# A recurrent attention with two expert layers: scans two chunks ahead, the last gate as three and one, and weight splits placed elsewhere

## Chip, core and metric

The kernel runs on one core of a Trainium2 chip, in one launch. The metric is the time of one execution on the device in microseconds, lower is better; the time given is the median of the runs, with the lowest and the highest beside it.

## The reference

Three layers follow each other. First a recurrence over 768 tokens for each of 4 batches and 8 heads of 48 channels:

```python
for t in range(S):
    cur = einsum('bhd,bhe->bhde', u * k[t], v[t])
    y[t] = einsum('bhd,bhde->bhe', r[t], state + cur)
    state = w[t] * state + einsum('bhd,bhe->bhde', k[t], v[t])
```

Its output is taken as 3072 tokens of 384 values. Each token whose skip score is positive goes through one of 8 experts, the one with the largest logit, and the result is scaled by the softmax weight and added:

```python
h = maximum(x[mask] @ w1[e], 0)          # 384 -> 1024
out[mask] = x[mask] + gate_w * (h @ w2[e])
```

A dense layer follows: `h = x @ w_in` (384 to 2048), `g = h * clip(h + 3, 0, 6) / 6`, `out = g @ w_out`.

## The kernel before

The order of each engine's instructions is written out by hand: what stands in the source is what the engine gets, in that order, and each engine works its own list from front to back, waiting where an input isn't ready or a buffer isn't free. There are three stages.

**The recurrence** works on 24 chunks (`NST`): 6 blocks of 128 tokens, 4 batches in each; chunk i is block i // 4 of batch i % 4. A loop over i holds in one step the work of several chunks:

- DVE: `state(i - 1)` updates the batch's state (lines 569 and 573, from the fifth step on), with the forward scan of a later chunk between its two lines (`scan`, line 431); then `scan_end`, `scan_inv` and four backward scans (`scan_back`, line 446); `masked(i + 1, 0)` and `(i + 1, 1)`, which mask the two groups of scores (line 494); the output add of chunk i in `x_out` (line 546, tile xt).
- POOL: `scale(i + 2)` multiplies r and k by the scanned weights (line 456, tile rkt); line 470 in `scale_rest`; the scatters of tokens to the experts' lists (line 663), of chunk i - 7.
- PE: `scores(i + 1)` (line 490, out of rkt), `apply(i)` in two halves (lines 524 to 534), with the transposes of chunk i - 1 between them (`xpose`), `k_xpose(i + 1)`, `state_mm(i)`, and the logits of chunk i - 1.
- ACT: copies, and `diag_v(i)`.

The state update reads the PSUM bank that the logits are written to as well, so it waits for the logits of the step before. Scores go to two banks, one for each group, and a group's next scores wait until the mask has read the last. Each block has a gate, in four functions: `gate_a` (six small instructions on DVE) and `gate_rank` (PE) in one step, `gate_o` and `gate_b` (DVE) in the next. The last block's gate runs as two halves of two chunks.

The experts' weights are split into a high part, which ACT rounds (`w_hi`, line 270), and a low part, which is the difference (`w_lo`, line 276). Twelve pieces of 128x768, the first expert's eight and four of the second's, are split within the recurrence: one in each of the steps 9 to 20, the low part on POOL. Raw pieces come in by DMA two steps ahead (`w_raw`).

**The experts**: for each of 8, eight pairs of `ffn1` and `ffn2`. A table of positions (`side_at`) places the splits of the coming expert between them, and work on the dense layer's weights: `d_words`, `d_bits`, `d_value`, `d_hi` and `d_lo` (line 327, on DVE). At the end of an expert, DVE adds its outputs to the tokens (line 855) and POOL scatters them back.

**The dense block**: 6 blocks of 512 tokens, PE without a gap.

Warm-up matmuls (`warm1`, line 394) fill PE at the start; their results are not used.

## Time and profile before

| what | before |
|---|---|
| median of 3 runs | 760.0 us (758.72 to 761.14) |
| the profiled execution | 762.69 us, span 761.0 us |
| mean granted clock of TensorE | 0.988 |
| PE busy | 734.3 us, 96% |
| DVE busy | 497.3 us, 65% |
| ACT busy | 346.9 us, 46% |
| POOL busy | 219.0 us, 29% |
| chain that ended last | PE 69%, DVE 21%, DMA 3% |

The share of busy time is a mean over three stages with different limits, and a busy PE is not one that PE's peak bounds, since the ends of matmuls are modelled. The chain of waits goes back from the last instruction, at each step to what released it; stretches of the timeline show who waited for whom in one place.

### The profile page before, as it was taken

The numbers are of one execution on the slowest core, as the hardware profiler recorded it, in microseconds if no ns is written. First come the engines' busy times: TensorE is split into PE (matmuls) and PEld (weight loads), VectorE is DVE, ScalarE is ACT, GpSimd is POOL, SyncE is SP. The second block draws the span as 40 slices with busy tenths as digits, with TensorE's granted clock in tenths as the row PEclk, the third lists the DMA queues.
The fourth block names the chain that finished last, engine by engine and source line by source line (L and its number), as shares of the span: only waits on it lengthen the run. The fifth ranks groups of instructions, "written<-read, shape, count | busy, mean of one in ns | idle before, by whom it ended". The sixth has DMA issues, their size and how long they took to land.

```text
span 761.0 us, 14589 instructions
## 1 busy us (share of the span) xinstructions
PE 734.3 (96%) x5653; PEld 604.8 (79%) x5653; DVE 497.3 (65%) x974; ACT 346.9 (46%) x796; POOL 219.0 (29%) x192
## 2 busy tenths in 40 slices
PE   7999999989999997989999999999999999999995
PEld 3788888859999997957777888888888888788884
DVE  8989999837999999927885454455445434333331
ACT  2666777626566666326554333333233333333331
POOL 3758999942344444303441000000000000000000
PEclk9999999999999999989999999999999999999998
DMA  8699888328787873042230220221022010001001
GB/s 233 206 300 264 246 243 251 112 86 287 249 276 238 288 250 143 13 159 62 85 103 13 77 68 13 79 66 37 2 90 67 25 54 1 1 0 43 0 1 46
DMA packets 40590, 90.84 MB, mean 119 GB/s; under 512 B 5442, under 2 KB 19552, under 8 KB 40512
## 3 DMA queue, kind: packets, MB, share of 16 engines
q1 hardware_dynamic: 37952, 85.14, 36.6%
q0 software_dynamic: 2560, 4.69, 1.7%
q8 instruction: 46, 0.75, 0.4%
q14 instruction: 32, 0.26, 0.1%
HBM read 72.51 MB, written 20.53 MB: 122 GB/s over the span
## 4 chain that ended last, share of the span: by engine, by line
PE 69%; DVE 21%; DMA 3%; ACT 2%; issue 2%; SPq 1%; POOL 0%; DVEq 0%; ACTq 0%
PE f L787 8%; PE f L788 8%; PE f L790 8%; PE acc L950 8%; PE acc L952 8%; PE acc L949 8%; DVE wlo L276 5%; PE sc L490 4%; PE x L534 3%; PE x L529 3%; PE x L524 2%; DVE wlo L327 2%; DVE hl L828 2%; DVE a L304 2%; DVE a L307 2%
## 5 line engine op out<-in xcount | busy, mean ns | idle before, releaser
L935 DVE SCALAR_TENSOR_TENSOR f<-t,f 128x512 f32<-128x512 f32 x96 | 66.6, 694 | 130.5 <-ACT t L934 130.5
L934 ACT ACTIVATE t<-f,three 128x512 f32<-128x512 f32 x96 | 66.0, 688 | 160.1 <-PE f L790 160.1
L950 PE MATMUL acc<-gh,wlo 128*128 128x512 f32 x288 | 115.0, 399 | 2.0 <-DVE wlo L327 1.8
L787 PE MATMUL f<-bh,whi 128*128 128x512 f32 x288 | 115.6, 401 | 0.6 <-ACT bh L922 0.6
L949 PE MATMUL acc<-gh,whi 128*128 128x512 f32 x288 | 115.7, 402 | 0.0
L788 PE MATMUL f<-bh,wlo 128*128 128x512 f32 x288 | 115.1, 400 | 0.0
L937 DVE TENSOR_TENSOR gl<-f,gh 128x512 fp32r<-128x512 f32 x96 | 66.4, 691 | 63.8 <-ACT gh L936 63.8
L936 ACT ACTIVATE gh<-f 128x512 fp32r<-128x512 f32 x96 | 57.4, 598 | 100.3 <-DVE f L935 100.3
L952 PE MATMUL acc<-gl,whi 128*128 128x512 f32 x288 | 84.0, 396 | 0.0
L790 PE MATMUL f<-bl,whi 128*128 128x512 f32 x288 | 83.6, 399 | 0.0
L950 PEld LDWEIGHTS acc<-gh,wlo 128*128 128x128 f32 x288 | 54.3, 188 | 17.5 <-DVE wlo L327 5.5
L314 POOL TENSOR_TENSOR lf<-lf,ab 128x384 f32<-128x384 f32 x32 | 32.5, 1015 | 121.0 <-DVE ab L308 100.1
L787 PEld LDWEIGHTS f<-bh,whi 128*128 128x128 f32 x288 | 54.9, 190 | 14.3 <-ACT bh L922 1.0
L276 DVE TENSOR_TENSOR wlo<-raw,whi 128x768 fp32r<-128x768 f32 x52 | 66.0, 1270 | 0.0
L788 PEld LDWEIGHTS f<-bh,wlo 128*128 128x128 f32 x288 | 55.0, 191 | 13.3
L790 PEld LDWEIGHTS f<-bl,whi 128*128 128x128 f32 x288 | 54.6, 190 | 13.4
L952 PEld LDWEIGHTS acc<-gl,whi 128*128 128x128 f32 x288 | 54.2, 188 | 13.2
L270 ACT ACTIVATE whi<-raw 128x768 fp32r<-128x768 f32 x64 | 54.1, 845 | 23.4 <-DMA raw<-in_wx_dram 23.1
L949 PEld LDWEIGHTS acc<-gh,whi 128*128 128x128 f32 x288 | 54.3, 189 | 11.8
L787 PE MATMUL f<-xh,whi 128*128 128x256 f32 x192 | 50.1, 290 | 6.1 <-DVE hl L828 5.3
L456 POOL TENSOR_TENSOR rkt<-ch,p 112x1024 f32<-112x1024 f32 x22 | 48.0, 2181 | 25.1 <-DVE p L446 14.3
L788 PE MATMUL f<-xh,wlo 128*128 128x256 f32 x192 | 48.7, 282 | 0.0
(149 smaller groups left out, 1410.9 us busy)
## 6 DMA issues: line engine op xcount, KB each, us to landing
raw<-in_wx_dram SPq DMA_DIRECT2D x64, 384.0 KB, 4.8
ch<-in_ch_dram SPq DMA_DIRECT2D x23, 674.2 KB, 5.9
draw<-in_wm_dram SPq DMA_DIRECT2D x32, 384.0 KB, 4.4
cw<-in_ch_dram SPq DMA_DIRECT2D x24, 226.2 KB, 2.6
v<-in_vt_dram SPq DMA_DIRECT2D x24, 192.0 KB, 3.9
xo<-xt SPq DMA_DIRECT2D x24, 192.0 KB, 3.2
xb<-xo SPq DMA_DIRECT2D x24, 192.0 KB, 3.8
out_dram<-y SPq DMA_DIRECT2D x17, 256.0 KB, 2.2
```

The source lines that it names most:

```text
L270: nc.scalar.activation(out=hi, in_=t, func=ACTF.Copy)
L276: (eng or nc.vector).tensor_tensor(out=lo, in0=t, in1=hi.bitcast(F32), op=ALU.subtract)
L787: nc.tensor.matmul(o, wh, xh, start=(i == 0), stop=False)
L788: nc.tensor.matmul(o, wl, xh, start=False, stop=False)
L790: nc.tensor.matmul(o, wh, xl, start=False, stop=(i == len(ws) - 1))
L934: nc.scalar.activation(out=t, in_=p, func=ACTF.Relu, bias=three)
L935: nc.vector.scalar_tensor_tensor(out=p, in0=t, scalar=6.0, in1=p, op0=ALU.min, op1=ALU.mult)
L936: nc.scalar.activation(out=hi, in_=p, func=ACTF.Copy)
L937: nc.vector.tensor_tensor(out=lo, in0=p, in1=hi.bitcast(F32), op=ALU.subtract)
L949: nc.tensor.matmul(acc[k][m], wh[:, os_[m]:os_[m] + 128], hi, start=(j == 0), stop=False)
L950: nc.tensor.matmul(acc[k][m], wl[:, os_[m]:os_[m] + 128], hi, start=False, stop=False)
L952: nc.tensor.matmul(acc[k][m], wh[:, os_[m]:os_[m] + 128], lo, start=False, stop=(j == 15))
```

## The change

**The look-ahead.** The loop starts at -2 instead of -3; where step i scanned chunk i + 3, it now scans chunk i + 2, whose product `scale(i + 2)` POOL makes in the same step. The block for `i == -1` with the scores of chunk 1 falls away; these scores now stand in step 0, behind the warm-up matmuls.

**The last gate.** `gate_a` and `gate_rank` of the last block run for three chunks in the last step, and the gate's rest for those three behind it; then a gate for the one chunk that is left. For that, the transposes of chunk 22, its logits and `gate_a` move ahead in the last step, and `diag_v` of the last chunk behind the transposes.

**The splits in the recurrence.** Six of the twelve stay on POOL, in the steps 9, 11, 13, 15, 17 and 19; the other six go to DVE, two in each of the steps 21, 22 and 23. The raw pool has five buffers instead of three.

**The splits of the dense weights.** For the first matrix the high and the low part of piece j come at position 52 + 2j/3 at the earliest, before at 50 + 4j/5.

```diff
@@ sizes
-W0 = 7
-            wpool["raw"] = p1.enter_context(tc.tile_pool(name="rawp", bufs=3))
+            wpool["raw"] = p1.enter_context(tc.tile_pool(name="rawp", bufs=5))
@@ in state
-                    if ok(i + 4):
-                        scan(i + 4)
+                    if ok(i + 3):
+                        scan(i + 3)
@@ in logits
-                b0 = 2 if i >= NST - 2 else 0
+                b0 = 3 if i == NST - 1 else 0
@@ in scatter
-                b0 = 2 if c == NCH - 1 and b >= 2 else 0
+                b0 = 3 if c == NCH - 1 and b == 3 else 0
@@ the table and the loop
-            rq = list(wq)
+            wat = {9 + 2 * k: ((wq[k], nc.gpsimd),) for k in range(6)}
+            wat.update({NST - 3 + k: tuple((p, nc.vector) for p in wq[6 + 2 * k:8 + 2 * k]) for k in range(3)})
-            for i in range(-3, NST + 1):
-                if i >= W0 + 2 and wq:
-                    w_hi(*wq[0])
-                if ok(i):
+            for i in range(-2, NST + 1):
+                for p, _ in wat.get(i, ()):
+                    w_hi(*p)
+                if ok(i) and i < NST - 1:
                     diag_v(i)
                 if ok(i - 1):
                     state(i - 1)
-                elif ok(i + 3):
-                    scan(i + 3)
-                if ok(i + 3):
-                    scan_end(i + 3)
-                    scan_inv(i + 3)
-                    if i + 3 > 0:
-                        scan_back(i + 3)
+                elif ok(i + 2):
+                    scan(i + 2)
+                if ok(i + 2):
+                    scan_end(i + 2)
+                    scan_inv(i + 2)
+                    if i + 2 > 0:
+                        scan_back(i + 2)
...
-                if i == -1:
-                    scores(1)
-                    for g in range(2):
-                        masked(1, g)
...
-                if i > 0 and ok(i + 1):
+                if i >= 0 and ok(i + 1):
                     scores(i + 1)
                     masked(i + 1, 0)
+                if i == NST - 1:
+                    xpose(i - 1)
+                    diag_v(i)
                 if ok(i):
                     apply(i, 0)
-                if ok(i - 1):
+                if ok(i - 1) and i != NST - 1:
                     xpose(i - 1)
-                if i >= W0 + 2 and wq:
-                    w_lo(*wq.pop(0), nc.gpsimd)
-                if i >= W0 and rq:
-                    w_raw(*rq.pop(0))
+                if i == NST - 1:
+                    logits(i - 1)
+                    gate_a(NCH - 1, 0, 3)
+                for p, eng in wat.get(i, ()):
+                    w_lo(*p, eng)
+                for p, _ in wat.get(i + 2, ()):
+                    w_raw(*p)
...
                 if i == NST - 1:
-                    logits(i - 2)
-                    gate_a(NCH - 1, 0, 2)
-                    logits(i - 1)
-                elif ok(i - 1) and i < NST - 2:
+                    gate_rank(NCH - 1, 0, 3)
+                elif ok(i - 1) and i < NST - 1:
                     logits(i - 1)
...
-            gate_rank(NCH - 1, 0, 2)
-            gate_o(NCH - 1, 0, 2)
-            gate_b(NCH - 1, 0, 2)
+            gate_o(NCH - 1, 0, 3)
+            gate_b(NCH - 1, 0, 3)
             logits(NST - 1)
-            for b in range(2):
+            for b in range(3):
                 scatter(NCH - 1, b)
             warm1(4, "sc0")
             for f in (gate_a, gate_rank, gate_o, gate_b):
-                f(NCH - 1, 2, 2)
-            for b in range(2, B):
-                scatter(NCH - 1, b)
+                f(NCH - 1, 3, 1)
+            scatter(NCH - 1, 3)
@@ in the experts' table
-                hi_at = max(50 + 4 * j // 5, at + 3) if m == 0 else max(58 + j, at + 3)
+                hi_at = max(52 + 2 * j // 3, at + 3) if m == 0 else max(58 + j, at + 3)
```

The changed kernel has one line fewer at its head, so its line numbers are one lower up to the loop (430 for 431, and so on). Its order on the engines, at three places:

DVE at the start, from the masks of chunk 1's scores (at) on; the four rows from line 431 are one chunk's scan, xt is the output add of chunk 0. Before:

```order
L494 TENSOR_TENSOR at<-sc_259,mask 128x4x128
L494 TENSOR_TENSOR at<-sc_260,mask 128x4x128
L431 SCALAR_TENSOR_TENSOR p<-ch,cb 112x516
L436 TENSOR_SCALAR cb<-p 112x4
L439 RECIPROCAL p<-cb 112x4
L446 SCALAR_TENSOR_TENSOR p<-ch,p,cb 112x127 x4
L546 TENSOR_TENSOR xt<-x,dv 128x384
```

and in the changed kernel:

```order
L493 TENSOR_TENSOR at<-sc_284,mask 128x4x128
L493 TENSOR_TENSOR at<-sc_285,mask 128x4x128
L545 TENSOR_TENSOR xt<-x,dv 128x384
L430 SCALAR_TENSOR_TENSOR p<-ch,cb 112x516
L572 TENSOR_TENSOR st_149<-sl,pc 112x192
L435 TENSOR_SCALAR cb<-p 112x4
L438 RECIPROCAL p<-cb 112x4
L445 SCALAR_TENSOR_TENSOR p<-ch,p,cb 112x127 x4
```

The scan of chunk 3 stood ahead of the add of chunk 0 and now stands behind it, around the state update (572). From here on, each scan's place holds the chunk before the one that it held; the rows as such read the same.

DVE in step 21, between the output adds (xt) of chunks 20 and 21; the rows from mx to od are the first half of a gate, at the masks of chunk 22's scores. Before:

```order
L546 TENSOR_TENSOR xt<-x,dv 128x384
L494 TENSOR_TENSOR at<-sc_2811,mask 128x4x128
L606 TENSOR_REDUCE mx<-sl 128x4
L608 SCALAR_TENSOR_TENSOR cb<-sl,desc 128x32
L612 TENSOR_TENSOR dl<-sl,mx 128x32
L617 SCALAR_TENSOR_TENSOR cd_153<-dl,cb 128x4x8
L620 TENSOR_REDUCE cb<-cd_153 128x4
L622 TENSOR_TENSOR od<-cd_153,cb 128x36
L494 TENSOR_TENSOR at<-sc_2812,mask 128x4x128
L546 TENSOR_TENSOR xt<-x,dv 128x384
```

and in the changed kernel, from the last backward scans of chunk 23 on:

```order
L438 RECIPROCAL p<-cb 112x4
L445 SCALAR_TENSOR_TENSOR p<-ch,p,cb 112x127 x4
L493 TENSOR_TENSOR at<-sc_2789,mask 128x4x128
L275 TENSOR_TENSOR wlo<-raw,whi 128x768 x2
L605 TENSOR_REDUCE mx<-sl 128x4
L607 SCALAR_TENSOR_TENSOR cb<-sl,desc 128x32
L611 TENSOR_TENSOR dl<-sl,mx 128x32
L616 SCALAR_TENSOR_TENSOR cd_153<-dl,cb 128x4x8
L619 TENSOR_REDUCE cb<-cd_153 128x4
L621 TENSOR_TENSOR od<-cd_153,cb 128x36
L493 TENSOR_TENSOR at<-sc_2790,mask 128x4x128
L545 TENSOR_TENSOR xt<-x,dv 128x384
```

Chunk 23's scan, which stood a step earlier, now opens the step, and two splits (wlo) stand between the two masks. Steps 22 and 23 hold two splits each in the same way; in step 23 they stand ahead of the last output add.

DVE in the experts, behind the additions of the sixth expert's tokens; hl is the low part of an activation, wlo from raw an expert's weights, wlo from wv the dense layer's. Before:

```order
L276 TENSOR_TENSOR wlo<-raw,whi 128x768
L828 SCALAR_TENSOR_TENSOR hl<-f_4922,hh 128x256
L327 TENSOR_TENSOR wlo<-wv_3167,whi 128x384
L327 TENSOR_TENSOR wlo<-wv_3168,whi 128x384
L276 TENSOR_TENSOR wlo<-raw,whi 128x768
L302 TENSOR_SCALAR a<-draw 128x384
L304 SCALAR_TENSOR_TENSOR a<-draw,a 128x384
L307 SCALAR_TENSOR_TENSOR a<-ab,a 128x384
L308 TENSOR_SCALAR ab<-a 128x384
L828 SCALAR_TENSOR_TENSOR hl<-f_4962,hh 128x256
```

and in the changed kernel:

```order
L275 TENSOR_TENSOR wlo<-raw,whi 128x768
L827 SCALAR_TENSOR_TENSOR hl<-f_4918,hh 128x256
L275 TENSOR_TENSOR wlo<-raw,whi 128x768
L301 TENSOR_SCALAR a<-draw 128x384
L303 SCALAR_TENSOR_TENSOR a<-draw,a 128x384
L306 SCALAR_TENSOR_TENSOR a<-ab,a 128x384
L307 TENSOR_SCALAR ab<-a 128x384
L827 SCALAR_TENSOR_TENSOR hl<-f_4953,hh 128x256
L275 TENSOR_TENSOR wlo<-raw,whi 128x768
```

The first two splits out of wv have gone from here; they come behind the transposed tokens of the next expert, two positions later than before.

## Rows read from the trace of the kernel before

**Rows 1.** Busy by stretch: us, PE PEld DVE ACT POOL busy (instructions), clock, DMA.

```profile
140.00:160.00 20.00, 19.89 (x384) 16.38 (x381) 12.67 (x38) 11.53 (x43) 15.88 (x15) 1.00 0.22 77
...
200.00:220.00 20.00, 20.00 (x145) 19.83 (x144) 19.69 (x33) 13.39 (x27) 8.97 (x9) 1.00 0.84 275
```

**Rows 2.** Chain of waits, PE's scores of chunks 9, 10, 11, 22, 23: start, us.

```profile
65.07 1.09 PE sc L490 x16
...
71.18 1.09 PE sc L490 x16
...
77.72 1.09 PE sc L490 x16
...
145.92 1.16 PE sc L490 x14
...
151.40 1.09 PE sc L490 x16
```

**Rows 3.** DVE in time order, steps 8 to 11: start, us, [idle before].

```profile
65.12 0.37 DVE L569 TENSOR_TENSOR cb<-sl,st 112x192 f32<-112x192 f32 x1 [0.29 <-PE sl L597]
...
67.52 1.59 DVE L446 TENSOR_TENSOR_SCAN p<-ch,p,cb 112x127 f32<-112x127 f32 x4
...
71.23 0.37 DVE L569 TENSOR_TENSOR cb<-sl,st 112x192 f32<-112x192 f32 x1 [0.48 <-PE sl L597]
...
77.78 0.35 DVE L569 TENSOR_TENSOR cb<-sl,st 112x192 f32<-112x192 f32 x1
...
84.55 0.35 DVE L569 TENSOR_TENSOR cb<-sl,st 112x192 f32<-112x192 f32 x1
```

**Rows 4.** POOL in time order, the same steps.

```profile
63.34 2.17 POOL L456 TENSOR_TENSOR rkt<-ch,p 112x1024 f32<-112x1024 f32 x1 [2.03 <-PE x L534]
...
69.25 2.18 POOL L456 TENSOR_TENSOR rkt<-ch,p 112x1024 f32<-112x1024 f32 x1 [1.07 <-PE x L529]
```

**Rows 5.** PE, then DVE, then POOL in time order, the start.

```profile
14.36 2.15 PE L490 MATMUL sc<-rkt 48*128 48x128 f32 x16 [2.05 <-DVE at L494]
...
23.36 1.16 PE L490 MATMUL sc<-rkt 48*128 48x128 f32 x16
...
19.17 1.22 DVE L431 TENSOR_TENSOR_SCAN p<-ch,cb 112x516 f32<-112x516 f32 x1
...
22.35 0.53 DVE L546 TENSOR_TENSOR xt<-x,dv 128x384 f32<-128x384 f32 x1
...
18.16 2.18 POOL L456 TENSOR_TENSOR rkt<-ch,p 112x1024 f32<-112x1024 f32 x1 [7.73 <-DVE p L446]
```

**Rows 6.** DVE, then POOL in time order, the recurrence's last adds and scatters.

```profile
155.71 0.56 DVE L546 TENSOR_TENSOR xt<-x,dv 128x384 f32<-128x384 f32 x1 [0.77 <-PE x L534]
...
159.25 0.56 DVE L546 TENSOR_TENSOR xt<-x,dv 128x384 f32<-128x384 f32 x1 [2.98 <-PE x L534]
...
162.60 0.97 POOL L663 DMA_INDIRECT xs<-xt,si  x1 [3.71 <-issue]
...
166.44 0.97 POOL L663 DMA_INDIRECT xs<-xt,si  x1 [0.30 <-issue]
```

**Rows 7.** Line 276 by engine: count, ns min/median/max, first and last start.

```profile
L276 DVE TENSOR_TENSOR wlo<-raw,whi x52: 939/1264/1769, 180.2 to 302.4; 128x768 fp32r<-128x768 f32 x52
...
L276 POOL TENSOR_TENSOR wlo<-raw,whi x12: 1819/1831/1840, 73.9 to 144.8; 128x768 fp32r<-128x768 f32 x12
```

**Rows 8.** DVE, then POOL in time order, around 6 us.

```profile
6.29 1.49 DVE L456 TENSOR_TENSOR rkt<-ch,p 112x512 f32<-112x512 f32 x1
...
5.97 1.26 POOL L470 TENSOR_TENSOR ru<-ch 112x512 f32<-112x512 f32 x1 [1.60 <-DMA ch<-in_ch_dram]
```

**Rows 9.** PE's waits in the experts, one stretch's clock, DVE's last add.

```profile
PE f L787 <- DVE hl L828: 5.3, 4, 2.8
...
302.00:306.00 4.00, 4.00 (x20) 3.82 (x19) 4.00 (x7) 0.80 (x2) 1.30 (x2) 0.57 0.00 0
...
323.83 0.62 DVE L855 SCALAR_TENSOR_TENSOR x<-acc,xw 128x384 f32<-128x384 f32 x1 [0.97 <-PE acc L850]
```

More of the change, by code (lines that the diff above doesn't have):

```diff
@@ L575, in state @@
                     nc.scalar.activation(out=sbd[b][64:112, :, D:2 * D], in_=st[b][64:112], func=ACTF.Copy)
-                elif ok(i + 4):
-                    scan(i + 4)
+                elif ok(i + 3):
+                    scan(i + 3)
             def xpose(i):
@@ L615, in gate_a @@
                 nc.scalar.activation(out=ex, in_=dl, func=ACTF.Exp)
-                cd = cdt[(c + b0 // 2) % 2][:, 0:nb, :]
+                cd = cdt[(c + b0 // 3) % 2][:, 0:nb, :]
                 nc.vector.scalar_tensor_tensor(out=cd[:, :, 0:E], in0=dl, scalar=0.0, in1=dk,
@@ L680, in rwkv_moe_kernel @@
                     state(i - 1)
-                elif ok(i + 3):
-                    scan(i + 3)
-                if ok(i + 3):
-                    scan_end(i + 3)
-                    scan_inv(i + 3)
-                    if i + 3 > 0:
-                        scan_back(i + 3)
-                if i == -3:
+                elif ok(i + 2):
[5 more added lines that the diff above has]
+                        scan_back(i + 2)
+                if i == -2:
                     for a in (0, 2):
@@ L692, in rwkv_moe_kernel @@
                     scale_rest(0)
-                if i == 1 - 3:
+                if i == 1 - 2:
                     scale(1)
@@ L712, in rwkv_moe_kernel @@
                         scatter(NCH - 2, b)
-                if i < 2 - 3:
-                    load_ch(i + 3 + 3)
+                if i < 2 - 2:
+                    load_ch(i + 2 + 3)
                 if ok(i + 5) and i >= 0:
@@ L733, in rwkv_moe_kernel @@
                     gate_b((i - 6) // 4, 0, B)
-                if i > 0 and ok(i + 1):
+                if i >= 0 and ok(i + 1):
                     masked(i + 1, 1)
@@ L756, in rwkv_moe_kernel @@
                         in_=zrow[:, None, :].to_broadcast([128, CAP // 128, XR])))
-                for k in range(1, i + 6) if i == -3 else (i + 5,):
+                for k in range(1, i + 6) if i == -2 else (i + 5,):
                     if ok(k):
                         load_v(k)
-            gate_rank(NCH - 1, 0, 2)
-            gate_o(NCH - 1, 0, 2)
-            gate_b(NCH - 1, 0, 2)
+            gate_o(NCH - 1, 0, 3)
+            gate_b(NCH - 1, 0, 3)
             logits(NST - 1)
-            for b in range(2):
+            for b in range(3):
                 scatter(NCH - 1, b)
```

## The prediction

> **What bounds the kernel now.** I first read the busy time by stretches, then the chain of waits, then each engine's instructions in time order in the places that the diff touches. The program has three stages: the recurrence to about 167 us, the experts to about 324, and the dense block, in which PE works without a gap and which the diff leaves alone. In the expert stretch DVE is busy for 19.69 of 20 us [rows 1], and so it stays up to the last rows of the stage: DVE is the bound there. In the recurrence PE is. It starts the scores of chunk 9 at 65.07, of chunk 10 at 71.18, of chunk 11 at 77.72 [rows 2]: 6.11 us for a plain step, 6.54 for one in which the rank matmuls of a gate stand too, and no PE wait between. Call T(i) the start of step i, in which PE first takes the scores of chunk i+1. In the last steps of the recurrence neither is full: DVE works 12.67 of 20 us [rows 1].
>
> DVE runs along with PE. The state update opens its step, and it waits for the logits, PE's last work of the step before (the releaser is named in the row at 65.12); 3.99 us after that start the backward scan ends, at 69.11 [rows 3]. POOL then multiplies the scanned weights into r and k, from 69.25 for 2.18 us [rows 4]. POOL's multiplications begin with chunk 2 (0 and 1 are DVE's), so the one at 63.34 is chunk 10's and the one at 69.25 chunk 11's. Chunk 11's ends at 71.43; PE wants it at 77.72. Today each product lies finished for some six microseconds.
>
> **The change, part by part.** The sum is made on the profiled execution, 762.69 us (span 761.0); it stands 2.69 over the median of 760.0, and I carry the difference over unchanged.
>
> *A, the start.* The scan of chunk 3, 3.18 us from 19.17 to the output add at 22.35 [rows 5], goes behind the add of chunk 0. PE's own order changes too: the five warm-up matmuls that follow chunk 1's scores now stand ahead of them, where PE sat idle for 2.05 us before 14.36. With the warm-ups inside that wait, chunk 2's scores come earlier than 23.36, but not ahead of POOL's product, which ends at 20.34 as before, since DVE's work up to it is the same. So the gain lies between 2.05 (just the wait filled) and 2.8 (product plus a handover). I take 2.5. In the first four steps nothing takes it back: there DVE's scan does not wait for logits, so the product stays ahead of PE. The numbers of A are in [rows 5].
>
> *B, the shorter look-ahead.* From step 5 on, DVE's rows stand where they stood, but each scan is for a chunk one earlier. The slot at 69.25 to 71.43 makes chunk 10's product, and PE wants that at 71.18: a wait replaces six microseconds of slack. Step by step: DVE starts at D(i) = the later of the logits' end of step i-1 and its own end; the product is ready at R(i) = D(i) + 3.99 + 0.14 + 2.18 = D(i) + 6.31; and T(i+1) is the latest of T(i) + 6.11 (6.54 in steps 5, 9, 13, 17), of R(i) + 0.1, and of the end of the second mask. DVE's own step takes 5.5 us when plain (6.11 between the starts at 65.12 and 71.23, less the waits), 6.55 in a gate's first step (71.23 to 77.78) and 6.77 in its second (77.78 to 84.55) [rows 3]. Without the R term these sums put chunk 22's scores at 145.87, and the trace has 145.92 [rows 2]. With it they come at 149.68: 3.8 us late, some 0.9 of it in the last step before, where PE has less to do. With no handover it is 3.4, with 0.3 us it is 4.6. I take 3.8, since DVE's handover to POOL is 0.14 [rows 3, 4].
>
> *C, six splits from POOL to DVE.* POOL's split takes 1.83 us, DVE's 0.94 at best, 1.26 in the median and 1.77 at worst [rows 7]. POOL's time was not on the path (that slack), so taking six off it gains nothing but a little inside B. On DVE they stand in steps 21, 22 and 23, two in each, ahead of the second mask or of the output add, for which PE waits: at(22), then at(23), then x of chunk 22, then x of chunk 23. Walking the rows in the new order, before A is taken off: scan of 23 up to 151.2, first mask, two splits (2.7, since POOL multiplies beside them), the gate's six rows (1.0, the 6.55 less 5.5), second mask, so that chunk 23's scores start at 156.2 (now 151.40 [rows 2]); two splits of 0.94 in each of the next steps, and the adds of chunks 22 and 23 start at 161.5 and 167.6 (now 155.71 and 159.25 [rows 6]). The fourth scatter of the last gate then starts at 173.35, now 166.44. The same walk without the splits gives 168.65, so C is 4.7 of their 6.2 us; 1.5 fall into waits that DVE has anyway. Bounds: 4.1 with all six at 0.94, and 5.9 when the product of chunk 23 comes between the two splits of step 21.
>
> The trace shows such a meeting once: half of chunk 0's product on DVE takes 1.49 us from 6.29, while POOL multiplies from 5.97 to 7.23 [rows 8], and it ends half a microsecond after POOL. The Trainium skill has this as a rule (SBUF — State Buffer, Who interferes with whom): a DVE instruction with two SBUF inputs and a GpSimd instruction that reads SBUF share a port pair as an exclusive lock, and one waits for the whole of the other. That row agrees. By the rule taken at its fullest one split of step 21 waits out POOL's product, and the sum below would be 765.6 instead of 764.4.
>
> *D, three and one.* Today the first scatter of the last gate starts 3.35 us after the last add (159.25 to 162.60), and four follow at 1.28 us up to 166.44 [rows 6]. With the three older chunks' first gate half done before that add, about 1.0 us of DVE work and a rank go from behind it. The fourth scatter falls behind the three others on POOL, not behind its own gate, by my walk 0.6 us. 168.65 less 166.44 less B's 3.8 is a gain of 1.6; if the single chunk's gate is the last to be ready after all, 0; at best 1.9.
>
> *E, the experts' splits.* The diff moves DVE's splits of the dense weights a position or two later, none away. DVE has no gap in the stage, so the last add (323.83 [rows 9]) moves only with the stage's start: 0. The deeper raw buffers give 0 too; no wait for a raw tile stands on these chains.
>
> Sum: -2.5 + 3.8 + 4.7 - 1.6 = +4.4; 762.69 becomes 767.1, the median **764.4 us**.
>
> **Rivals.** *1, faster: the experts' last part follows PE.* PE waits there for the activations' low half, 5.3 us in all [rows 9], because splits stand ahead of it on DVE, and afterwards its granted clock is 0.57 over 302 to 306 [rows 9], the lower of its two levels (1.2 GHz) for most of that stretch; four microseconds at half speed cost two. If the later splits remove both and the stage's end follows, 7.3 us go: 764.4 - 7.3 = 757.1. It decides as soon as the last add at 323.83 keeps its distance to PE's work rather than to DVE's. Against it: DVE works through all of this, and the same rows stand ahead of its last activation.
>
> *2, no change: the splits cost nothing.* DVE's free 7 us in 140 to 160 [rows 1] take them in. Then C is 0: 759.7. Against it: these free times are waits for PE, and the splits stand ahead of what PE waits for.
>
> *3, slower still: splits and gate both at their worst.* C 5.9, D 0, B 4.6: with A at 2.5 that is +8.0, so 768.4. It happens when POOL's product and the splits meet and the single gate ends last.
>
> *4, the start gives nothing*, because the warm-ups, moved, delay chunk 1's scores by as much: A is 0, 766.9. Against it: the wait of 2.05 us is as long as the warm-ups.
>
> **How the numbers follow.** Forecast 0.52, rival 1 0.10, rival 2 0.15, rival 3 0.16, rival 4 0.07. A measurement of this kernel tells about 0.3% from no change, so 757.7 to 762.3 is the same. Faster is rival 1: 0.10. The same is rival 2 and the forecast's thin lower edge (its bounds together give +2.8, 762.8): 0.18. Slower: 0.72. The range leaves out rival 1 and a little beyond rival 3: 758.0 to 769.0.
>
> **What would show it.** A: PE's scores of chunk 2 near 20.5 to 21, with no full stop before chunk 1's. B: from step 6 on PE waits for POOL's rkt at the head of plain steps, about a third of a microsecond each, and POOL's rkt ends just before each group of scores instead of a step ahead. C: L275 rows on DVE in three pairs after 145, PE waiting for DVE's masks and adds between them. D: three scatters starting about 1.8 us after the last add, the fourth behind them. E: the distance from the first expert matmul to the last add unchanged within 1 us. I am wrong if chunk scores keep a step of 6.11 (then the product is not last), or if the splits start in DVE's waits.

## The result, and the profile after

The changed kernel takes 771.12 us (median of 4 runs, 766.56 to 774.21) where the kernel before takes 760.57 in the same measurement: ratio 1.0122, 95% interval 1.0085 to 1.0158. By the medians that is 10.5 us slower, by the ratio on record 9.3 us, where +4.4 was forecast; 771.12 lies above the range's end of 769.0. Measured again later the ratio was 1.0102 (1.0062 to 1.0141), 7.8 us. The four runs of the changed kernel had mean granted clocks of 0.990, 0.984, 0.982 and 0.972, the shortest run the highest. The kernel before took 760.6, 766.2, 766.4, 767.0, 760.9 and 761.3 us in the six measurements of this study, so kernels are compared as ratios to it within one measurement; a thousandth is 0.77 us. In e8 below, three of the twelve runs were in a slower state and are not in its ratio.

The profiled execution of the changed kernel is its shortest, 766.56 us with a span of 764.9. Its page, and the engines' busy time:

```profile
span 764.9 us, 14577 instructions
PE 732.6 (96%) x5653; PEld 601.4 (79%) x5653; DVE 505.6 (66%) x980; ACT 347.5 (45%) x796; POOL 209.3 (27%) x186
...
PE 48%; DVE 25%; issue 3%; DMA 3%; ACT 2%; POOL 0%; SPq 0%; DVEq 0%; ACTq 0%; POOLq 0%
```

PE is 1.7 us less busy in a span that is 3.9 us longer, and the chain that ended last now lies on PE for 48% of the span, before for 69%. PE in time order, the scores of chunks 2, 8, 13, 21, 22 and 23 (start, duration, in brackets the idle time before and what ended it):

```profile
20.28 1.16 PE L489 MATMUL sc<-rkt 48*128 48x128 f32 x16
...
55.73 1.25 PE L489 MATMUL sc<-rkt 48*128 48x128 f32 x16 [0.24 <-POOL rkt L455]
...
88.36 1.16 PE L489 MATMUL sc<-rkt 48*128 48x128 f32 x16 [0.49 <-POOL rkt L455]
...
140.13 1.16 PE L489 MATMUL sc<-rkt 48*128 48x128 f32 x16 [1.16 <-POOL rkt L455]
...
146.52 1.16 PE L489 MATMUL sc<-rkt 48*128 48x128 f32 x16 [1.34 <-POOL rkt L455]
...
155.88 2.08 PE L489 MATMUL sc<-rkt 48*128 48x128 f32 x16
```

Chunk 2's scores come 3.08 us earlier than in [rows 5]. From chunk 8 on PE waits for POOL's product, 4.9 us in nine waits: seven of 0.22 to 0.49 us at plain steps, of which two stand here, and the two long ones ahead of chunks 21 and 22. By chunk 22 the 3.08 are gone, and 1.11 more: 146.52 against 145.41 in the kernel before, whose row in time order is

```profile
145.41 1.66 PE L490 MATMUL sc<-rkt 48*128 48x128 f32 x16
```

(The row at 145.92 in [rows 2] is the last 14 of these 16 matmuls, where the chain of waits enters the group.) Chunk 23's scores then come 4.5 us late, and last 2.08 us instead of about 1.1. DVE and POOL in time order show why they are late:

```profile
148.16 0.67 DVE L493 TENSOR_TENSOR at<-sc,mask 128x512 f32<-128x512 f32 x1
148.74 4.56 DVE L275 TENSOR_TENSOR wlo<-raw,whi 128x768 fp32r<-128x768 f32 x1
...
155.09 0.68 DVE L493 TENSOR_TENSOR at<-sc,mask 128x512 f32<-128x512 f32 x1
...
162.07 0.55 DVE L545 TENSOR_TENSOR xt<-x,dv 128x384 f32<-128x384 f32 x1
...
167.88 0.55 DVE L545 TENSOR_TENSOR xt<-x,dv 128x384 f32<-128x384 f32 x1
```

```profile
149.09 2.17 POOL L455 TENSOR_TENSOR rkt<-ch,p 112x1024 f32<-112x1024 f32 x1
151.23 1.25 POOL L469 TENSOR_TENSOR ru<-ch 112x512 f32<-112x512 f32 x1
152.65 1.56 POOL L662 DMA_INDIRECT xs<-xt,si  x1 [0.17 <-issue]
...
169.97 0.97 POOL L662 DMA_INDIRECT xs<-xt,si  x1 [3.87 <-issue]
...
173.80 0.97 POOL L662 DMA_INDIRECT xs<-xt,si  x1 [0.30 <-DVE cum L658]
```

The first split of step 21 stands on DVE for 4.56 us. POOL multiplies from 149.09 to 152.48, first the product rkt, then ru; the split ends at 153.30, 0.82 behind ru. The second mask follows at 155.09, and PE has had nothing to do. The stretches (as in [rows 1]: length, PE, PEld, DVE, ACT, POOL busy, granted clock, DMA) show what that does:

```profile
150.00:152.00 2.00, 1.21 (x40) 1.12 (x36) 2.00 (x1) 0.38 (x1) 2.00 (x2) 1.00 0.00 0
152.00:154.00 2.00, 0.00 (x0) 0.00 (x0) 2.00 (x2) 0.00 (x0) 1.83 (x2) 0.69 0.00 0
154.00:156.00 2.00, 1.36 (x20) 1.27 (x20) 1.90 (x9) 1.47 (x4) 1.19 (x2) 0.50 0.79 206
156.00:158.00 2.00, 2.00 (x17) 1.78 (x18) 0.35 (x3) 2.00 (x9) 0.00 (x0) 0.50 0.51 189
...
170.00:172.00 2.00, 2.00 (x11) 0.77 (x9) 0.87 (x6) 0.21 (x1) 1.70 (x2) 0.50 0.17 59
```

PE is idle for all of 152 to 154, and behind that its granted clock is 0.50, the lower of its two levels (1.2 GHz), while chunk 23's scores run; so again at 170, behind the wait for the last add. The last scatter starts at 173.80, 7.4 us later than in [rows 6]. Of this the span shows only 3.9, mainly because the kernel before ran the start of its dense block at the lower level in its profiled execution and the changed kernel did not. The same view of the kernel before, then of the changed one:

```profile
332.00:336.00 4.00, 2.71 (x9) 1.89 (x10) 1.12 (x3) 0.98 (x2) 0.00 (x0) 0.63 1.01 339
336.00:340.00 4.00, 4.00 (x11) 3.09 (x11) 0.25 (x1) 0.69 (x1) 0.00 (x0) 0.52 0.31 124
```

```profile
340.00:344.00 4.00, 3.28 (x16) 2.54 (x17) 1.15 (x3) 0.89 (x2) 0.00 (x0) 1.00 0.97 310
344.00:348.00 4.00, 4.00 (x19) 3.21 (x18) 2.08 (x3) 2.33 (x4) 0.00 (x0) 1.00 0.39 157
```

From the dense block's first matmul to the end the kernel before takes 426.3 us, the changed one 423.2.

### The profile page after: what moved, and what is told of

It reads as the page before. It is cut to its first block, busy times and chain, and to the rows that moved or that the text cites. A ratio compares the mean times of both kernels' runs of the same rounds, so it can differ in the third digit from the quotient of the medians.

```text
span 764.9 us, 14577 instructions
## 1 busy us (share of the span) xinstructions
PE 732.6 (96%) x5653; PEld 601.4 (79%) x5653; DVE 505.6 (66%) x980; ACT 347.5 (45%) x796; POOL 209.3 (27%) x186
## 4 chain that ended last, share of the span: by engine, by line
PE 48%; DVE 25%; issue 3%; DMA 3%; ACT 2%; POOL 0%; SPq 0%; DVEq 0%; ACTq 0%; POOLq 0%
PE acc L949 8%; PE acc L951 8%; PE acc L948 8%; DVE wlo L275 8%; PE f L786 8%; PE f L789 7%; PE f L787 7%; DVE hl L827 3%; DVE wlo L326 2%; DVE a L303 2%; DVE a L306 2%; DVE f L934 1%; DVE a L301 1%; DVE gl L936 1%; ACT gh L935 1%
## 5 line engine op out<-in xcount | busy, mean ns | idle before, releaser
L275 DVE TENSOR_TENSOR wlo<-raw,whi 128x768 fp32r<-128x768 f32 x58 | 74.2, 1284 | 0.0
```

The lines of the kernel that those rows point to most:

```text
L275: (eng or nc.vector).tensor_tensor(out=lo, in0=t, in1=hi.bitcast(F32), op=ALU.subtract)
```

## Experiments

Each ratio is to the kernel before in the same measurement. "Filled" means that warm-up matmuls stand in PE's waits.

| run | kernel | ratio | 95% interval |
|---|---|---|---|
| e4 | before + look-ahead and start | 1.0064 | 1.0041 to 1.0087 |
| e9 | e4 + waits filled | 1.0052 | 1.0031 to 1.0073 |
| e13 | e4, four scatters out | 1.0077 | 1.0042 to 1.0112 |
| e3 | before + splits on DVE | 1.0021 | 0.9996 to 1.0046 |
| e7 | before + gate | 0.9998 | 0.9974 to 1.0023 |
| e1 | changed, splits back on POOL | 1.0075 | 1.0049 to 1.0101 |
| e2 | changed, splits later | 1.0057 | 1.0031 to 1.0083 |
| e6 | changed, again | 1.0102 | 1.0062 to 1.0141 |
| e10 | changed, waits filled | 1.0055 | 1.0032 to 1.0078 |
| e16 | e1, waits filled | 1.0027 | 1.0004 to 1.0050 |
| e18 | e2, waits filled | 1.0044 | 1.0022 to 1.0067 |
| e8 | before + start's order + gate | 1.0014 | 0.9976 to 1.0052 |
| e15 | before + start's order, filled | 0.9990 | 0.9967 to 1.0012 |
| e17 | e15 + gate | 0.9984 | 0.9960 to 1.0009 |
| e11 | before, waits filled | 1.0031 | 1.0005 to 1.0057 |
| e12 | before, four scatters out | 0.9961 | 0.9938 to 0.9983 |
| e14 | before, scatters spread | 1.0021 | 0.9997 to 1.0044 |

### One part at a time

**e4, the look-ahead and the start alone**: the part of the diff that the prediction calls B, and the start that goes with it.

```diff
-                    if ok(i + 4):
-                        scan(i + 4)
+                    if ok(i + 3):
+                        scan(i + 3)
...
-            for i in range(-3, NST + 1):
+            for i in range(-2, NST + 1):
```

> The kernel before with only the shorter look-ahead (and the order of the start that goes with it). Theory: chunk 2's scores 3.1 us earlier, as in the changed kernel's trace, and the waits for POOL's product take 3.7 us back by chunk 22's scores: 760.5 to 761.5. Rival: with POOL's splits in every step 9 to 20 its product comes later still, and the look-ahead alone costs 3 us or more: 763 or more.

4.9 us slower: the rival's size. Yet up to chunk 22's scores the trace is close to the theory: from chunk 2's to chunk 22's it is 126.4 us, against 122.1 in the kernel before (23.36 to 145.41), so the look-ahead takes 4.3 us, 3.1 of which the start gives.

**e3, the splits alone**, in the kernel before:

```diff
-            rq = list(wq)
+            wat = {9 + 2 * k: ((wq[k], nc.gpsimd),) for k in range(6)}
+            wat.update({NST - 3 + k: tuple((p, nc.vector) for p in wq[6 + 2 * k:8 + 2 * k]) for k in range(3)})
```

> The kernel before with only the move of the six splits to DVE (and five raw buffers). Here chunk 23's weights are scanned a step earlier, so POOL's product of chunk 23 is done before DVE reaches the splits of step 21. Theory: without the meeting a split takes 0.9 to 1.3 us, and the move costs 2.5 to 4.5 us: median 762.5 to 764.5. Rival 1: the move costs the same here as in the changed kernel, 7 us or more: 767 or more. Rival 2: nothing, because DVE has free time in these steps: 760.

1.6 us (-0.3 to 3.5), between nothing and the theory. Its trace has the shortest meeting, DVE's split beside POOL's ru (DVE, then POOL, in time order):

```profile
149.28 1.54 DVE L276 TENSOR_TENSOR wlo<-raw,whi 128x768 fp32r<-128x768 f32 x1
```

```profile
148.73 1.28 POOL L470 TENSOR_TENSOR ru<-ch 112x512 f32<-112x512 f32 x1
150.17 1.57 POOL L663 DMA_INDIRECT xs<-xt,si  x1 [0.16 <-issue]
```

ru ends at 150.01, the split 0.81 later, and the scatter that is issued meanwhile takes 1.57 us instead of the usual 1.0.

**e7, the gate alone**, in the kernel before:

```diff
-                f(NCH - 1, 2, 2)
-            for b in range(2, B):
-                scatter(NCH - 1, b)
+                f(NCH - 1, 3, 1)
+            scatter(NCH - 1, 3)
```

> The kernel before with only the last gate as three chunks and one. Theory (the term D of the sum): 1.6 us less, between 0 and 1.9, so a ratio of 0.9975 to 1.0. Rival: the four scatters of the block before and the three of the last now stand closer together and PE waits more in the last step, so that the clock falls there: slower by 1 to 3 us.

No change: neither the gain of 1.6 nor the rival's loss, though the interval (-2.0 to +1.8 us) holds most of both. The mean granted clock of its runs is 0.983, that of the kernel before in the same measurement 0.985.

**e1, the splits back on POOL**, in the changed kernel:

```diff
-            wat = {9 + 2 * k: ((wq[k], nc.gpsimd),) for k in range(6)}
-            wat.update({NST - 3 + k: tuple((p, nc.vector) for p in wq[6 + 2 * k:8 + 2 * k]) for k in range(3)})
+            wat = {9 + k: ((wq[k], nc.gpsimd),) for k in range(12)}
```

> The changed kernel with the twelve splits of the recurrence back on POOL, one in each of the steps 9 to 20; look-ahead, gate and dense splits as changed. Theory: the six splits on DVE are the loss, above all the first of step 21, which stood on DVE for 4.56 us beside POOL's product and its next multiplication. Then the scores of chunk 23 come at about 152 us instead of 155.9, the last scatter of the last gate at 166 instead of 173.8, and the median is about 759 to 761. Rival 1: the shorter look-ahead is the loss, and the splits only make up what it has delayed: the median stays at 766 or more. Rival 2: the dense splits, or the clock in the later stages whatever the recurrence does, are the loss: the last scatter near 166, but the median still 765 or more.

5.7 us slower, rival 1's size: of the 7.8 to 9.3 us by which the two measurements put the changed kernel above the one before, the splits are only about 2.8, and the intervals of the two kernels leave 3 us of doubt on that. Chunk 23's scores come at 154.15, not at 152.

**e2, the splits later**:

```diff
-                for p, eng in wat.get(i, ()):
+                for p, eng in wat.get(i, ()) if i < NST - 3 else ():
                     w_lo(*p, eng)
...
                     x_out(i)
+                for p, eng in wat.get(i, ()) if i >= NST - 3 else ():
+                    w_lo(*p, eng)
```

> The changed kernel; DVE keeps its six splits, but in the steps 21, 22 and 23 the two splits stand behind the step's output add instead of ahead of the second mask. Theory: it is the place that costs, not the work, since behind the add of step 21 POOL has no product left to multiply and PE waits for nothing of DVE there: a split takes 0.9 to 1.3 us, chunk 23's scores come at 151 to 152.5 instead of 155.9, and the two splits of the last step, now behind the last add, cost up to 1.8 us of the gate: last scatter at 167 to 169, median 760 to 763. Rival: the splits cost DVE's time wherever they stand, some 4.7 us by my first sum: 765 or more.

1.0057, some 4 us less than the changed kernel: the place matters, as the theory said, but 4.4 us remain. Chunk 23's scores come at 152.88. The first split (at 153.09) met only ru and took 1.80 us.

### The clock

**e6, the changed kernel again**, and **e5, the kernel before again**, with no edit, on the same chip:

> The changed kernel, unchanged, measured again in many runs beside the kernel before and profiled once more. Theory: the ratio of the first measurement, 1.012, holds within its interval (1.008 to 1.016), and a slower execution shows more stretches at the lower clock between 140 and 180 us than the first trace, which had 6.83 us from 152.8 and 3.4 us from 169.8. Rival: on one chip the two kernels stand closer, 1.005 to 1.007 like the look-ahead alone, and the rest of the first ratio was the spread of the runs.

> The kernel before, unchanged, profiled on the chip of this call. In the four experiments so far PE pauses 3 to 5 us between matmuls of one group around 158 to 165 us, without a wait that the trace names, while POOL issues four to six scatters in a row, and its granted clock falls to the lower level there. Theory 1: that pause comes with the scatters, whatever the kernel, so that the kernel before shows it here too and the last scatter of the last gate comes at 170 or later instead of 166.4; then it is no part of the change. Theory 2: it needs PE's shorter or longer waits that the change brings: then the kernel before shows none, PE is busy for all of 150 to 160, and its last scatter stands at 166 to 167.

e6: 1.0102, the theory. The split took 4.12 us and ended 0.82 behind ru. e5: theory 1. The kernel before, too, pauses there and has the last scatter at 174.96. These pauses stood in 11 of the 12 traces of those three measurements in which the kernel before took 766 to 767 us, and in none of the 8 other traces, the changed kernel's first among them. They are no part of the change. Nor is every stretch at the lower level: between 135 and 180 us the kernel before has none in its first trace and 10.2 us in this one, the changed kernel 10.2 and 17.1; in the whole of the traces from 6 to 750 us the kernel before has 13.7 and 20.5, the changed kernel 10.2 and 20.5. What tells the two kernels apart is the mean of many runs: a granted clock of 0.985 (23 runs) against 0.981 (6 runs) in this measurement. PE in e1, where they were longest:

```profile
159.35 0.29 PE L506 MATMUL kp<-u_sb,ru 112*64 112x2 f32 x4 [0.40 <-issue]
160.78 0.32 PE L506 MATMUL kp<-u_sb,ru 112*64 112x2 f32 x4 [1.14 <-issue]
...
163.64 0.16 PE L506 MATMUL kp<-u_sb,ru 112*64 112x2 f32 x1 [1.03 <-issue]
```

"issue" is idle time for which the trace has no wait: inside one group of matmuls PE starts a few every 0.7 us.

**e10, the changed kernel, filled**:

```diff
+                if i in (20, 21):
+                    warm1({20: 5, 21: 6}[i])
                 if i >= 0 and ok(i + 1):
                     scores(i + 1)
...
+                if i == 21:
+                    warm1(14)
                 if i == NST - 1:
                     gate_rank(NCH - 1, 0, 3)
+                    warm1(8)
```

> The changed kernel with warm-up matmuls in PE's waits of the last steps: five ahead of chunk 21's scores, six ahead of chunk 22's, fourteen ahead of the rank matmuls of step 21 (PE waits 1.9 to 3.4 us there), eight behind the rank matmuls of the last step. Theory: as above, the clock stays at the upper level to 160 us, the last scatter comes 2 to 4 us earlier, and the ratio falls from 1.010 to about 1.005. Rival 1: no change, 1.010. Rival 2: the warm-ups stand in the way of the logits and scores and cost what they save.

The theory: 1.0055, about 4 us less than the changed kernel, with a mean granted clock of 0.991 over its runs where e6 has 0.981. Its trace at the same place, stretches as above:

```profile
152.00:154.00 2.00, 2.00 (x14) 0.92 (x12) 2.00 (x1) 0.00 (x0) 1.83 (x3) 1.00 0.00 0
154.00:156.00 2.00, 1.77 (x19) 0.90 (x17) 1.90 (x9) 0.58 (x3) 1.70 (x2) 1.00 0.33 41
156.00:158.00 2.00, 2.00 (x24) 1.64 (x24) 1.52 (x5) 2.00 (x7) 0.39 (x1) 1.00 0.71 263
```

Chunk 23's scores still come at 156.33, since DVE is as late as before; but PE is at the upper level (2.4 GHz) when they come, and stays there from 14 to 167.7 us.

The lists of runs allow a second estimate of what the clock costs. Among runs of one kernel in one measurement, each thousandth by which the mean granted clock is lower goes with 0.3 to 0.5 us (a straight line through the runs, with one slope for each measurement). The 4.5 thousandths between the two kernels in e6's measurement are then worth some 2 us of the 7.8, and at an equal clock the changed kernel would stand 5 to 6 us above the kernel before. This is an estimate from runs that differ in more than the clock, not an experiment. It also shows a limit of e10: its clock of 0.991 is compared with a kernel before that has 0.983 in that measurement, so the filling may remove stretches that the change did not bring.

**e9, the look-ahead alone, filled**, the kernel e4 with

```diff
+                if i in (20, 21, 22):
+                    warm1({20: 5, 21: 6, 22: 4}[i])
                 if i >= 0 and ok(i + 1):
                     scores(i + 1)
```

> The kernel with only the shorter look-ahead, and on PE five, six and four warm-up matmuls ahead of the scores of chunks 21, 22 and 23, about as long as PE's waits there (0.98 us, 1.3 and 0.94). They change no wait of another engine. Theory: the look-ahead costs more than its waits because TensorE's granted clock falls behind them (141.6 to 145.0 us in the trace without the filling, 148 to 152 in others); with the waits filled no stretch at the lower level begins between 138 and 150, chunk 22's scores come 1 us earlier or more in relation to chunk 8's, and the median is 2 to 4 us below the 1.0064 of the look-ahead alone: 1.001 to 1.004. Rival: the clock is no part of it, the waits themselves are the loss: 1.006 again.

The rival, mostly: 0.9 us less than e4, which the intervals don't tell from nothing. In e4 the clock falls behind the wait for chunk 21's product, and in e9 it doesn't (e4, then e9):

```profile
140.00:142.00 2.00, 1.02 (x20) 0.93 (x18) 1.91 (x4) 0.00 (x0) 2.00 (x2) 0.89 0.96 345
142.00:144.00 2.00, 2.00 (x17) 1.44 (x14) 1.90 (x7) 1.55 (x5) 1.82 (x3) 0.50 0.52 184
```

```profile
140.00:142.00 2.00, 2.00 (x22) 1.28 (x20) 1.90 (x5) 0.83 (x2) 1.85 (x3) 1.00 0.97 351
142.00:144.00 2.00, 2.00 (x41) 1.60 (x41) 2.00 (x6) 2.00 (x10) 1.97 (x2) 1.00 0.24 81
```

But chunk 22's scores come no sooner, 126.6 us behind chunk 2's: they wait for POOL's product, and POOL for DVE's scan, whatever PE's clock. The lower level costs there nothing, and 4.0 us remain.

**e16 and e18, filled, with the splits on POOL or later**: the edits of e1 and of e2 with e9's.

> The changed kernel with all twelve splits back on POOL, and with five, six and four warm-ups ahead of the scores of chunks 21 to 23: look-ahead and gate as changed, the clock held. Beside the changed kernel with its waits filled (1.0055) it gives the price of the six splits on DVE without the clock's part. By my sum that price is 4.7 us and the ratio here is 0.999 to 1.000. Rival: the splits cost little once the clock is held, since the filled look-ahead alone already stands at 1.005: 1.004 to 1.006.

> The changed kernel with the two splits of the steps 21, 22 and 23 behind the step's output add, and with five, six and four warm-ups ahead of the scores of chunks 21 to 23. Theory: with the clock held, the place of the splits shows: without the wait for POOL's two multiplications ahead of chunk 23's scores some 2.5 us less than the changed kernel with filled waits (1.0055), so 1.002 to 1.003, about as with the splits on POOL (1.0027). Rival: 1.005 or more, since the splits delay the last gate instead.

e16, 1.0027, lies between theory and rival; in its trace no stretch between 6 and 753 us is at the lower level, and the last scatter stands at 167.30. It takes 3.7 us less than e1. Against e10 the splits cost 2.1 us with the waits filled (give or take 2.5). e18, 1.0044, lies between too, 1.0 us below e2 and 0.8 below e10, neither of them clear of the noise; its split stood beside POOL's ru again, for 1.97 us.

### The scatters

**e12**, and **e13** with e4's edit too, leave out a loop of the last step; **e14** keeps it with clears between:

```diff
-                    for b in range(B):
-                        scatter(NCH - 2, b)
```

```diff
                         scatter(NCH - 2, b)
+                        for _ in range(3 if b < 3 else 0):
+                            nc.gpsimd.memset(gap, 0.0)
```

> The kernel before without the four scatters of the last block but one (the tokens of chunks 16 to 19 do not reach the experts' lists; all else runs). It asks where PE's pauses of 0.7 us come from that stand between 156 and 165 us in six of ten traces, in both kernels, while POOL issues four to six scatters in a row. Theory: they come with that row of scatters; without it no pause stands there, and the time is 2 to 4 us lower. Rival: they come without the scatters as well, with what else the last steps do: pauses as before, time as before.

> The kernel with only the shorter look-ahead, without the four scatters of the last block but one (the tokens of chunks 16 to 19 do not reach the experts' lists). In its traces POOL issues six scatters in a row from 155 to 163 us, where the kernel before issues two, waits, and issues four; PE's unexplained pauses add up to 2.4 to 4.5 us in the kernels with six in a row, to 1.1 to 2.5 in the others. Theory: this is what the look-ahead costs beyond its 1.3 us by my sum; without the scatters the kernel stands 1.3 us above the kernel before without them (ratio 0.996 then), so at 0.997 to 0.999. Rival: the cost is elsewhere, and it stands 4 us above, at 1.001 to 1.002.

> The kernel before, with three clears of a small tile (0.4 us each) on POOL between each two of the four scatters of the last block but one, so that they start 2.5 us apart instead of 1.28. Theory: the pauses come with the closeness of the scatters: fewer pauses between 155 and 165 us and 1 to 3 us less, ratio 0.996 to 0.999. Rival 1: they come with the scatters as such: the same pauses, spread out, ratio 1.000. Rival 2: the later scatters are in the way of the last gate's and cost 1 us or more.

Without the scatters (e12) the kernel before had no pause in a measurement in which the three other traces had them, and took 3.0 us less. That they make the look-ahead's cost fell: e13, the look-ahead without them, stood at 1.0077, although leaving them out alone gave 0.9961. Its times reach from 763.0 us, at a mean granted clock of 0.993, to 773.9 at 0.976. e14 tells nothing of the pauses, since none of the traces of its measurement has them; spread, the scatters gain nothing.

### What is left as a gain

All in the kernel before: **e8**, the start's warm-ups ahead of chunk 1's scores, and e7's gate; **e15**, that order without the gate, and three warm-ups ahead of chunk 3's scores; **e17**, order, warm-ups and gate; **e11**, `warm1(4)` ahead of the rank matmuls of step 21 and of the logits of the last step. The order and its filling:

```diff
             for i in range(-3, NST + 1):
+                if i == 0:
+                    scores(1)
+                    for g in range(2):
+                        masked(1, g)
...
-                if i == -1:
-                    scores(1)
-                    for g in range(2):
-                        masked(1, g)
...
+                if i == 2:
+                    warm1(3)
                 if i > 0 and ok(i + 1):
                     scores(i + 1)
```

> The kernel before with the last gate as three and one, and with the five warm-up matmuls of the start ahead of chunk 1's scores instead of behind them; the scans stay three chunks ahead. Theory (A without B, and D): the wait of 2.05 us ahead of chunk 1's scores is filled, with no product that comes late afterwards, and the gate gives 1.6 us: 3 to 4 us less than before, ratio 0.995 to 0.996. Rival: the start gives nothing, since chunk 1's scores then come as much later: the same ratio as the gate alone.

> The kernel before with the five warm-ups of the start ahead of chunk 1's scores, and three more ahead of chunk 3's, where the trace of that start order with the last gate showed a wait of 0.64 us and behind it 13.65 us at the lower granted clock (28.5 to 42.1 us), while PE had no gap. Theory: the short wait sets off that stretch; with it filled the clock stays up, the start's 3 us are kept, and the runs no longer fall into two groups: ratio 0.996. Rival: the stretch has nothing to do with the wait: two groups of runs again, ratio 1.000 or above.

> The kernel before with what the experiments left as gains: the start's five warm-ups ahead of chunk 1's scores, three warm-ups ahead of chunk 3's, and the last gate as three and one; scans three ahead and splits on POOL as before. Theory: chunk 23's scores 2.5 us earlier (150.1 against a mean of 152.6 in the traces of the kernel before), and 0.7 us from the gate: ratio 0.996 to 0.998, runs in one group. Rival: the start alone gave 0.999 and the gate alone 1.000, so what the start saves is lost again behind chunk 23, and this gives 0.999 to 1.000 too.

> The kernel before with four warm-up matmuls ahead of the rank matmuls of step 21 and four ahead of the logits of the last step, where its second trace shows PE waiting 0.93 us and the granted clock at the lower level from 153.3 to 160.1. Theory: part of the kernel's usual 766 us is that stretch; filled, 1 to 3 us go: ratio 0.996 to 0.999. Rival: the stretch comes from the pauses that no wait explains, and filling changes nothing: 1.000.

e8 stands at 1.0014, where 0.995 to 0.996 was forecast; its times reach from 761.4 to 775.0 us. PE in its trace (span 771.8), then the stretches behind, then one of them in e15:

```profile
27.23 1.97 PE L490 MATMUL sc<-rkt 48*128 48x128 f32 x16 [0.64 <-DVE at L494]
```

```profile
28.00:32.00 4.00, 4.00 (x36) 2.73 (x35) 3.93 (x11) 1.39 (x6) 2.46 (x3) 0.56 0.97 280
...
36.00:40.00 4.00, 4.00 (x37) 2.99 (x34) 3.01 (x9) 2.76 (x12) 0.72 (x1) 0.50 0.94 280
```

```profile
36.00:40.00 4.00, 4.00 (x83) 3.48 (x84) 3.93 (x10) 2.74 (x11) 3.57 (x4) 1.00 1.03 287
```

Behind one wait of 0.64 us the clock is at the lower level from 28.5 to 42.1 with PE busy throughout. With the wait filled (e15) no such stretch stands there, and the times reach from 757.5 to 765.0; but that was another measurement, and 0.9990 is no gain that can be told. e17 has chunk 23's scores at 150.00 and the last scatter at 164.38, both ahead of [rows 2, 6], and at 0.9984 (0.9960 to 1.0009) it is the fastest of those that leave nothing out; that it beats the kernel before is not shown. e11 fell: it costs 2.4 us.

## Why the prediction was wrong

The sign was right, the size was not. By its terms:

**A, the start, was right in kind** and a little short: chunk 2's scores come 3.08 us earlier in the first traces and 3.2 in the mean (at 21.2 in the ten traces with the look-ahead, at 24.4 in the seven with the old start), against 2.5 (up to 2.8). Of the 3.08, 0.35 stand already in chunk 0's scores (7.48, before 7.83), which is no part of A. The trace of before has the clock at the lower level from 15.6 to 19.0, behind the wait of 2.05 us [rows 5]; the changed kernel's first trace has none at the start, and the sum left that out. Rival 4 falls.

**B, the look-ahead, was right where it was worked out.** To chunk 22's scores it takes 4.2 us in the first traces (1.11 late, 3.08 early before) and 4.3 in e4, against 3.8; the waits stand where the recurrence had put them, for POOL's product. The 0.4 between is a reading: the walk's 149.68 was set against 145.92 [rows 2], while the group starts at 145.41, and 149.68 less that is 4.3. That the sums without the product's term gave 145.87 was thus no confirmation to 0.05 us.

**C, the splits, failed in its first row.** The walk gave the pair of step 21 2.7 us and, at most, one wait for POOL's product. It took 5.43, since the split waited for the product and for ru, the next instruction on POOL, and so chunk 23's scores came 2.2 us behind the walk (155.88; 156.2 less A's 2.5 is 153.7), and the last scatter 2.95 (173.80 against 170.85). The Trainium skill's rule (SBUF — State Buffer, Who interferes with whom) of an exclusive lock on the shared port pair holds in this trace; but where the rule, at its fullest, made the split wait for one instruction of POOL, it waited here for two, 4.56 us instead of 0.94. As a price at the end C is nevertheless smaller than 4.7: 2.8 (changed kernel less e1), 1.6 alone (e3), 2.1 with the waits filled (e10 less e16). Each of these is within its noise of nothing; together they make 2.0, give or take 1.4. Rival 2's price of nothing is about as near to that as the forecast's 4.7, but its time of 759.7 is not what came. Rival 3's mechanism, the meeting of product and split, is what happened.

**D, the gate**: the last scatter starts 5.92 us behind the last add, before 7.19 [rows 6], so 1.3 of the forecast 1.6 are in the trace; the three scatters start 2.09 behind the add and the fourth behind them, as walked. In the time of e7 nothing is left of it, at a granted clock that is lower by 2.5 thousandths; whether that hides the gain is not shown.

**E** is 0: from the first expert matmul to the last scatter of outputs it is 151.7 us in the mean of the traces with the changed table and 151.7 in those without. Rival 1 falls.

Two of the prediction's sums are off without touching the forecast or the range: rival 3 comes to 768.0 rather than 768.4, and the six splits are 6.5 us (2.7 and four of 0.94), not 6.2.

**Two steps failed. The first is the sum of A and B, 1.3 us in the forecast.** The two alone measure 4.9 us (e4), 4.0 with the waits filled (e9) and 5.9 in a kernel without the four scatters (e13). Chunk 23's scores come only 0.9 us later (153.6 in the mean of the three traces, 152.7 in six with the order of before up to there): 3 us or more arise behind them. The clock is not shown to be their cause, since e9 held it up to 159 and kept them, and the row of scatters isn't (e13). What it is stays open.

**The second is one that all terms shared: the sum held the clock fixed.** It was added to one execution of the kernel before, and the waits of B and C were priced at their own length. Behind these waits TensorE runs at 1.2 GHz in the changed kernel's last steps, in each execution in other places: 10.2 us in all between 135 and 180 in its first trace, 17.1 in the second, whose span is 7.6 us longer. With the waits filled the change costs 4.2 us (e10) instead of 7.8 to 9.3, and e1 falls by 3.7 (e16); but e4 falls by only 0.9 and e2 by 1.0, and the run lists give the clock some 2 us. So 1 to 4 us of the loss are put down to the clock, by argument from these numbers and not by an experiment that changes the clock alone. That 4.2 is what the sum had is luck in part, by errors that cancel: A, B and D measure 2.1 together where the sum had -0.3 (e16), C 2.1 where it had 4.7. The range had no end for the clock.

## What to carry to other kernels

Where one engine works without a gap at its upper clock, a wait put on it can cost more than its length: look in the profile for what the granted clock does behind each of its present waits, and put that beside the wait. When an instruction that reads two tiles of SBUF moves to DVE, write down what POOL runs at that moment and all that follows there without a gap, since it may wait for the whole row. Where a kernel's executions differ by more than the change, one trace is one draw; take the times of several and read the clock with them.

## What the runs showed that was not expected

A split on DVE that meets POOL's multiplications ends 0.81 to 0.83 us behind the last one of the row, in six traces: after 4.56, 4.12 and 4.58 us where the row is two (the changed kernel twice, e10), after 1.97, 1.80 and 1.54 where it is one (e18, e2, e3). In the two longest cases it is recorded as started 0.35 us ahead of POOL's product, in the other 0.10 behind it, and in all three ru, too, went ahead of it.

The lower clock level lasted 13.65 us with PE busy throughout, behind a wait of 0.64 us (e8, in one execution).

PE started its matmuls a few at a time every 0.7 us, with pauses of 0.7 to 3.8 us in all, and no wait in the trace (11 traces). That came and went between measurements, in both kernels, and its cause stays open.
